# Retention followed by a Fourier-mix block: residual of two row blocks on VectorE, their rows earlier, and two loads placed behind the first weight

## The chip, the cores and the metric

The kernel runs on one core of a Trainium2 chip. The metric is device microseconds of one execution, as the median of the runs. The core's engines are named here as the profile names them: TensorE (PE, and PEld for its weight loads), VectorE (DVE), ScalarE (ACT), GpSimd (POOL), and SyncE (SP), which issues most of the DMAs. Each engine works through its own instructions in order and waits on semaphores of the others.

## The reference

Four batches of 768 rows; eight heads of 64 columns make rows of 512. The first half is a decaying linear attention, the second a Fourier mix with a normalisation and a two-layer network, all in float32:

```python
for t in range(S):                                   # attention, per head h, gamma[h]
    state = gamma * state + outer(k[t], v[t])
    y[t] = scale * q[t] @ state
x = heads of y side by side                          # [4, 768, 512]
X = np.fft.fft(np.fft.fft(x, axis=1), axis=2)
u = x + np.real(X)                                   # the residual x is added here
un = (u - mean(u)) / sqrt(var(u) + 1e-6)             # over the 512 columns
out = u + np.maximum(un @ w_ch1, 0) @ w_ch2          # 512 -> 2048 -> 512
```

## The kernel before

A batch is worked in this order: load and cast q, k, v by head pairs; transposes, scores, state and outputs of the attention, which fill `x` (float16, 768 rows as six chunks of 128); the Fourier transform over rows (stage one, giving four tables `g`), then over columns (stage two), which gives `u` for six row blocks of 128 rows, called row blocks 0 to 5 here (`kb` in the code). Row blocks 3 to 5 come from reversed copies of the tables, `g16r` (units `gr0` to `gr3`). Then each row block is normalised (`bn_stats`, `bn_aggr`, then `un = mean - u`), transposed to `unT`, and goes through the network: `psh = w1 * unT`, relu into `ht`, `psc = ht * w2`, and `ob = psc * (1/std) + u`, which is stored.

The first batch has code of its own, since nothing runs beside its beginning. Its instructions are emitted in the order of the string `FIRST`, and `pin()` makes each engine keep that order. The tokens that matter here:

- `sa<r><part>`: the stage-two matmuls of row block r (r = 0, 1, 2) into one PSUM tile `pq0`. Part 0, 2 and 3 multiply the tables; part 1 adds the residual x by two matmuls with an identity matrix.
- `ua<r>`: takes `pq0` out of PSUM to `u`, adding the per-row constant `g0` (L929 on ScalarE, L931 on VectorE).
- `bn<r>` (L953, L954) and `n<r>` (L963, on ScalarE): statistics and `un`. Row block 0 has a shortcut: its mean is known beforehand, so `nh0`, `nh1` (L943) make `un` straight from PSUM, `pt0`, `pt1` (L975) transpose it and `pe0`, `pe1` (L981) copy it to `unT`.
- `g0`, `g1`, `g2`: the three steps of the constant `g0` (DVE L874 and L882; nine small matmuls L891; DVE L897 and L900). `csn0` is a table copy that the nine matmuls need (L355).
- `ge01`, `ge11`: the last two tables `g` out of PSUM (L837). `gr0` to `gr3`: the reversed copies (L863, VectorE).
- `fs3`: the last fold of x (DVE L760), read by the stage-one matmuls `s011`, `s111` (L827).
- `w0` to `w7`: issue of the eight weight loads on GpSimd's queue, four for w_ch1 (L1144), four for w_ch2 (L1151). The loads for q, k and v go through SyncE's queue (L215 for the first batch, L195 for later ones).

Behind the first batch's string, units are merged by due times. For row blocks 0 to 2 of the first batch the up-projection is done per row block in four groups of 16 matmuls (`h0_unit`, L1104). I write (r, g) for group g of row block r. Each group fills one of three PSUM buffers (pool `ps_pm`), which is emptied by relu (L1111 on ScalarE for even g, L1113 on VectorE for odd g). Before row blocks 1 and 2 stands `unT_unit` (transposes L1074, copy L1076 on VectorE or L1078 on ScalarE). On ScalarE the eight scaled masks for later batches (L277, `late_consts`) are issued behind the last `un` of `FIRST`. Stage two of row blocks 3 to 5 (`s2_unit`: matmuls L1025 and L1028, ScalarE copy L1030, VectorE L1031 and L1033, residual on GpSimd L1037 and L1039), their statistics (L1049, L1050) and `un` (L1051) run among these groups. The down-projection (`psc`, L1130) uses the same three PSUM buffers.

The loads of q for the first two head pairs of the second batch are issued at the head of the program, directly behind the first batch's twelve loads:

```python
for name, i in LOADS0:
    first_load(name, i, nc.sync)()
load_unit(1, 0, None, "q")()
load_unit(1, 1, None, "q")()
```

The other loads of the second batch wait for weight load `w6` and for the last matmul of (1, 3).

Of the kernel before, what the change touches and what calls it, by code (L numbers as in the profile page):

```python
# [18 lines left out]
P = 128  # L19
# [19 lines left out]
yi11 t21 sc1 ae110@v yi10 fs0 fl2@g yx1 q3 s110 w0 k31@g e21@a x10@v am20 am21 x11@a fs1 ta40  # L39
v22@a s010 k30@a t30 e30@a t31 v21@g e31@a ae201@v ta30 ae200@v kv2 ae211@v yi21 ae210@v gk2@g  # L40
sc2 csn2@a w1 csn1@v am30 ae300@v ta31 yi20 yx2 v32@g x20@a ae301@v xs0@v x21@a ta41 fl3@a gk3@g
s100 am31 ae311@v s000 v31@g kv3 fs2 s101 ge10@a ae310@v w2 s001 w3 yi31 sc3 ge00@a yi30 yx3 g0
x30@a sa00 sa10 edge x31@v fs3 w4 gr0 sa11 csn0@v s011 xs2@a xs3@v w5 s111 xs1@a sa20 mean
ge01@a sa02 sa01 ge11@v sa03 nh0@a gr3 sa12 nh1@a gr1 sa13 g1 sa21 pt0 g2 ua1@v pt1 sa22 pe0@a
pe1@a w6 ua0@v bn1 sa23 ua2@a gr2 n1 bn2 n2 w7
"""
ON_ACT = {'q': (0, 1, 0), 'kv': (1, 1, 1), 'g': (0, 1, 1), 'gr': (0, 0, 0)}
FB = 1
# [13 lines left out]
def kernel(  # L62
# [122 lines left out]
    def load_unit(b, i, after=None, names="qkv"):  # L185
        def run():
            h0 = 2 * PAIR_ORDER[i]
            for name in names:
                if (name, b, i) in in_of:
                    continue  # L190
                src = srcs[name]
                t = inp.tile([P, 2, NCH, D], f32, tag="in32", name=f"{name}32")
                rows = "h (p c) d -> p h c d" if b < NPE and name == "q" else \
                    "h (c p) d -> p h c d"
                dma = nc.sync.dma_start(t, src[b, h0:h0 + 2].rearrange(rows, p=P))  # L195
                if after is not None:
                    for x in (w_dma[after].ins, lb[0]["mm"].ins):
# [19 lines left out]

    for name, i in LOADS0:
        first_load(name, i, nc.sync)()
    load_unit(1, 0, None, "q")()  # L220
    load_unit(1, 1, None, "q")()


    icol_i = const.tile([P, 8], i32, tag="icol_i")
# [679 lines left out]
    lb = {}  # L904

    def sa_unit(kb, part):
        def run():
            if part == 0:
                if 0 not in lb:
                    lb[0] = dict(u=up.tile([P, NCH, DM], f32, tag="u32", name="u32"),  # L910
                                 unT=up.tile([P, 4, S], f16, tag="unT", name="unT"),
                                 st=stt.tile([P, NCH, 4], f32, tag="stats", name="stats"))
                lb[0]["pq", kb] = ps_g.tile([P, DM], f32, tag="g", name="pq0")
            pq, g, x = lb[0]["pq", kb], fd[0]["g"], xts[0][:, kb]
            sl = slice(kb * P, kb * P + P)
            ops = (((g[:, 0, sl], cd16[:, 0], 0, DM), (g[:, 2, sl], sd16[:, 0], 0, DM)),
                   ((ident16, x[:, 0, 1:257], 0, 256), (ident16, x[:, 1, 257:1:-1], 256, DM)),
                   ((g[:, 1, sl], cd16[:, 1], 0, DM),),
                   ((g[:, 3, sl], sd16[:, 1], 0, DM),))[part]
            for n, (lhsT, rhs, c0, c1) in enumerate(ops):  # L920
                nc.tensor.matmul(pq[:, c0:c1], lhsT, rhs, start=(part == 0 and n == 0),  # L921
                                 stop=part == 3, skip_group_check=True)
        return run

    def ua_unit(kb, eng):
        def run():
            dst, src, g0 = lb[0]["u"][:, kb], lb[0]["pq", kb], fd[0]["g0"][:, kb:kb + 1]
            if eng == "a":
                nc.scalar.activation(dst, src, AF.Identity, bias=g0, scale=1.0)  # L929
            else:  # L930
                nc.vector.tensor_scalar(out=dst, in0=src, scalar1=g0, scalar2=0.0, op0=ALU.add,  # L931
# [162 lines left out]
                                        op0=ALU.mult, op1=ALU.max)  # L1094
        return run

    def h0_unit(kb, g):
        def run():
            unT = lb[0]["unT"]
            psh = ps_pm.tile([P, 4, P], f32, tag="pm", name="psh0")  # L1100
            for f in range(4):
                fb = 4 * g + f
                for cb in range(4):
                    mm = nc.tensor.matmul(psh[:, f], w116[:, cb, fb * P:(fb + 1) * P],  # L1104
                                          unT[:, cb, kb * P:(kb + 1) * P],
                                          start=(cb == 0), stop=(cb == 3))
# [81 lines left out]
    def first_unit(name):  # L1188
# [16 lines left out]
            return x0_unit(n[0], n[1], eng or "a")  # L1205
        if kind == "ge":
            return s1e_unit(n[0], n[1], eng or "a")
        if kind == "nh":
            return n0_unit(n[0], eng or "a")
        if kind == "pe":  # L1210
# [33 lines left out]
    def mix_units(b, kbs, s0, s1, u0, u1):  # L1244
        def turn(j):
            def run():
# [5 lines left out]
        return [([turn(j) for j in range(3)], s0, s1), ([norm_unit(b, kbs[2])], t, t),  # L1252
                ([unT_unit(b, kb) for kb in kbs], u0, u1)]

    def emit(streams):
        ev = []
        for si, (units, t0, t1) in enumerate(streams):
# [18 lines left out]
    for b in range(B):  # L1276
        majors = []
        if b == 0:
            for kb in range(3):
                if kb:  # L1280
                    majors.append(unT_unit(0, kb))
                majors += [h0_unit(kb, g) for g in range(4)]
        else:
            majors += [h_unit(b, 0, fb) for fb in range(NFB)]
        majors.append(rstd_unit(b, 0))
# [56 lines left out]
```

## Time and profile before

| | |
|---|---|
| median of 3 runs (lowest to highest) | 242.21 us (242.10 to 242.36) |
| the profiled execution | 242.18 us, of which its span 240.4 us |
| PE busy | 228.3 us, 95% of the span |
| DVE busy | 173.4 us, 72% |
| ACT busy | 120.8 us, 50% |
| POOL busy | 82.8 us, 34% |
| DMA, mean rate | 153 GB/s, 36.77 MB |

The profile is of one execution. Times in its views are counted from the start of the span; what lies around the span (1.8 us here) isn't shown. A row of the timeline has the start, the duration, the engine, the source line and the operation with its tiles; in square brackets stands how long the engine had been idle before it and what it waited for.

### The profile page before, as it was taken

What the parts mean: (1) busy time and instruction counts of PE and PEld (TensorE: products, weight loads), DVE (VectorE), ACT (ScalarE), POOL (GpSimd) and SP (SyncE); (2) the same over time, 40 slices, a digit from 0 to 9 for tenths busy, and PEclk for the clock granted to TensorE, in tenths of its full rate; (3) what the DMA queues carried; (4) which work ended last, traced back from release to release, by engine and by line L of the source; (5) the groups of instructions that cost most, each with busy time, mean ns of one, the idle gap of its engine ahead of it and who ended that gap; (6) DMA issues with size and microseconds to landing.
All of it is one profiled execution on the core that took longest, in us unless ns stands there. A gap on an engine that the chain in (4) does not pass through costs nothing.

```text
span 240.4 us, 5243 instructions
## 1 busy us (share of the span) xinstructions
PE 228.3 (95%) x1999; PEld 142.5 (59%) x1999; DVE 173.4 (72%) x421; ACT 120.8 (50%) x268; POOL 82.8 (34%) x151
## 2 busy tenths in 40 slices
PE   0988999999999999999999999999999999999994
PEld 0466779766774756665567446655675455446542
DVE  8999887958898789977895749977886557215121
ACT  5989758675864544931148406722366227203400
POOL 7678802675300197840002808920004124000000
PEclk9999999999999999999999999999999999999999
DMA  7999999999999289979999488675100331221012
GB/s 181 231 271 238 236 206 208 215 248 246 260 215 230 47 197 218 179 144 146 256 277 208 103 174 213 131 109 153 46 0 0 90 109 24 43 90 45 0 44 87
DMA packets 100808, 36.77 MB, mean 153 GB/s; under 512 B 91440, under 2 KB 97840, under 8 KB 100784
## 3 DMA queue, kind: packets, MB, share of 16 engines
q1 hardware_dynamic: 96560, 32.25, 63.2%
q0 software_dynamic: 4224, 4.19, 10.5%
q8 instruction: 15, 0.25, 0.5%
q14 instruction: 9, 0.07, 0.1%
HBM read 27.26 MB, written 6.29 MB: 140 GB/s over the span
## 4 chain that ended last, share of the span: by engine, by line
PE 85%; DVE 4%; DMA 3%; POOL 2%; ACT 2%; SPq 1%; issue 1%; ACTq 0%
PE psc L1130 34%; PE psh L1087 28%; PE psh L1104 3%; PE wkA L664 3%; DMA v<-in_v_dram 3%; PE ps L847 3%; PE wkY L718 2%; PE pq L1009 2%; PE ps L827 1%; PE wkY L714 1%; PE wkK L683 1%; PE pq L921 1%; SPq L215 1%; PE tq L620 1%; POOL q16z L453 1%
## 5 line engine op out<-in xcount | busy, mean ns | idle before, releaser
L1130 PE MATMUL psc<-w,ht 128*128 128x512 f16 (+2 forms) x400 | 88.9, 370 | 0.0
L1087 PE MATMUL psh<-unT,w 128*128 128x384 f16 x448 | 81.6, 326 | 0.3 <-ACT ht L1091 0.3
L1130 PEld LDWEIGHTS <-ht 128*128 128x128 f16 x400 | 37.6, 98 | 36.7
L1087 PEld LDWEIGHTS <-w 128*128 128x128 f16 x448 | 42.1, 98 | 24.2 <-issue 0.8
L1091 ACT ACTIVATE ht<-psh 128x384 f16<-128x384 f32 x66 | 31.7, 490 | 41.2 <-PE psh L1087 40.6
L1037 POOL TENSOR_TENSOR u<-u,x 128x256 f32<-128x256 f32 x21 | 13.3, 635 | 107.8 <-DVE u L1016 95.6
L1134 DVE SCALAR_TENSOR_TENSOR ob<-psc,stats,u 128x512 f32<-128x512 f32 (+2 forms) x25 | 18.1, 725 | 29.2 <-PE psc L1130 29.0
L1093 DVE TENSOR_SCALAR ht<-psh 128x384 f16<-128x384 f32 x46 | 25.3, 550 | 8.9 <-PE psh L1087 8.4
L667 DVE TENSOR_TENSOR atm<-wkA,maskp 128x512 f16<-128x512 f32 x36 | 23.6, 681 | 1.5 <-PE wkA L664 1.5
L1051 ACT ACTIVATE un<-u,stats 128x512 f16<-128x512 f32 x21 | 14.9, 719 | 12.2 <-DVE stats L1050 8.2
L1049 DVE BATCH_NORM_STATS2 bst<-u 128x6 f32<-128x512 f32 x21 | 14.5, 688 | 4.9 <-POOL u L1039 4.7
L693 DVE SCALAR_TENSOR_TENSOR s<-s,gk,wkK 128x128 f16<-128x128 f16 x48 | 16.2, 337 | 2.4 <-ACT s L689 1.6
L726 ACT ACTIVATE x<-wkY,gexp 128x384 f16<-128x384 f32 x24 | 12.9, 581 | 9.0 <-PE wkY L718 8.9
L438 POOL TENSOR_SCALAR kd<-k,gexp 128x384 f16<-128x384 f32 x24 | 13.8, 586 | 3.3 <-DMA k<-in_k_dram 3.1
L664 PE MATMUL wkA<-qTz,kT 128*128 128x256 f16 x72 | 13.2, 272 | 0.1
L1039 POOL TENSOR_TENSOR u<-u,x 128x256 f32<-128x256 f32 x21 | 13.3, 635 | 0.0
L1011 ACT COPY qn<-pq 128x128 f32<-128x128 f32 x18 | 4.9, 274 | 13.7 <-PE pq L1009 13.7
L1104 PEld LDWEIGHTS <-w 128*128 128x128 f16 x192 | 11.0, 98 | 0.9 <-issue 0.6
L1104 PE MATMUL psh<-unT,w 128*128 128x128 f16 x192 | 11.4, 219 | 0.1
L1016 DVE SCALAR_TENSOR_TENSOR u<-pq,g,qn 128x256 f32<-128x256 f32 x18 | 8.5, 474 | 3.2 <-PE psh L1087 2.5
L443 POOL TENSOR_SCALAR v<-v 128x768 f16<-128x768 f32 x12 | 10.0, 832 | 1.6 <-DMA v<-in_v_dram 1.6
L664 PEld LDWEIGHTS <-kT 128*128 128x128 f16 x72 | 6.9, 98 | 5.7 <-issue 0.6
(177 smaller groups left out, 311.9 us busy)
## 6 DMA issues: line engine op xcount, KB each, us to landing
q<-in_q_dram SPq DMA_DIRECT2D x16, 384.0 KB, 6.1
k<-in_k_dram SPq DMA_DIRECT2D x16, 384.0 KB, 5.4
v<-in_v_dram SPq DMA_DIRECT2D x16, 384.0 KB, 6.0
out_dram<-ob SPq DMA_DIRECT2D x23, 256.0 KB, 2.4
w<-in_moe_w_ch_dram POOLq DMA_DIRECT2D x8, 512.0 KB, 10.9
unT<-un SPq DMA_TRANSPOSE x15, 2.4
out_dram<-ob SPq DMA_DIRECT2D x1, 192.0 KB, 1.9
kT<-kd SPq DMA_TRANSPOSE x10, 3.0
```

Of the source, the lines that this page charges most:

```text
L438: kc = nc.gpsimd.tensor_scalar(out=kd[:, :, h2, :], in0=k32[:, h2], scalar1=gkd[:, h0 + h2:h0 + h2 + 1], scalar2=1.0, op0=ALU.mult, op1=AL ...
L664: mm = nc.tensor.matmul(wk[:, c2], st["kT"][:, c, :], st["qT"][:, :, c, :], start=True, stop=True)
L667: nc.vector.tensor_tensor(out=st["atm"][:, 2 * part:2 * part + 2], in0=wk, in1=maskp[:, PAIR_ORDER[i]].unsqueeze(1).to_broadcast([P, 2, 2, ...
L693: nc.vector.scalar_tensor_tensor(out=s16[:, c], in0=s16[:, c - 1], scalar=gk2[:, hp:hp + 1], in1=wk[:, c - c0], op0=ALU.mult, op1=ALU.add)
L1049: nc.vector.bn_stats(bst, u[:, kb, :])
L1051: nc.scalar.activation(un, u[:, kb, :], AF.Identity, bias=stats[:, kb, 0:1], scale=-1.0)
L1087: nc.tensor.matmul(psh, w116[:, cb, fb * P:(fb + 1) * P], unT[:, cb, rt * 384:(rt + 1) * 384], start=(cb == 0), stop=(cb == 3))
L1091: nc.scalar.activation(ht16[:, fb, :], psh, AF.Relu, bias=0.0, scale=-1.0)
L1093: nc.vector.tensor_scalar(out=ht16[:, fb, :], in0=psh, scalar1=-1.0, scalar2=0.0, op0=ALU.mult, op1=ALU.max)
L1104: mm = nc.tensor.matmul(psh[:, f], w116[:, cb, fb * P:(fb + 1) * P], unT[:, cb, kb * P:(kb + 1) * P], start=(cb == 0), stop=(cb == 3))
L1130: nc.tensor.matmul(psc[:, c0:c1], ht16[:, fb, rb3 * P:(rb3 + 1) * P], w216[:, fb, c0:c1], start=(fb == 0), stop=(fb == NFB - 1))
L1134: nc.vector.scalar_tensor_tensor(out=ob[:, c0:c1], in0=psc[:, c0:c1], scalar=lb[b]["st"][:, rb, 3:4], in1=lb[b]["u"][:, rb, c0:c1], op0=AL ...
```

## The change

- Row blocks 1 and 2 of the first batch no longer get their residual by identity matmuls (`sa11` and `sa21` are gone from `FIRST`). `ua1` and `ua2` now are two `scalar_tensor_tensor` each on VectorE, of 128x256, which read PSUM, add `g0` and add x; the second reads x backwards. Row block 0 keeps the identity matmuls, and its `ua0` moves from VectorE to ScalarE, while `ua2` moves from ScalarE to VectorE.
- The order in `FIRST` is another: `csn0` and `g1` are earlier; `g2`, `sa12`, `sa13`, `ua1` and `bn1` come directly behind row block 0's last matmul; all four `gr` copies come at the end, behind `bn2`.
- `unT_unit(0, 1)` and `unT_unit(0, 2)` are emitted in the middle of the group before their row block (after two of its four parts), and a unit that does nothing keeps the count of units as it was. In the program that results, TensorE's order around the first three row blocks is: (0,0), (0,1), (0,2); transposes of row block 1; transposes of row block 2; two matmuls of row block 3's stage two; (0,3); four matmuls of row blocks 3 and 4; (1,0) to (1,3); (2,0); the other six matmuls of row blocks 4 and 5; (2,1) to (2,3). Before it was: (0,0), (0,1), (0,2); three transposes; (0,3); five transposes; all twelve matmuls of row blocks 3 to 5; (1,0) to (2,3). Later, in the second half of the first batch's network, some matmuls of the second batch's attention and of the network change places.
- The two early q loads of the second batch are no longer at the head of the program. They stand in `FIRST` as `lq02` and `lq13`: the first waits until weight load `w2` has landed, the second until `w3` has.

```diff
-s100 am31 ae311@v s000 v31@g kv3 fs2 s101 ge10@a ae310@v w2 s001 w3 yi31 sc3 ge00@a yi30 yx3 g0
-x30@a sa00 sa10 edge x31@v fs3 w4 gr0 sa11 csn0@v s011 xs2@a xs3@v w5 s111 xs1@a sa20 mean
-ge01@a sa02 sa01 ge11@v sa03 nh0@a gr3 sa12 nh1@a gr1 sa13 g1 sa21 pt0 g2 ua1@v pt1 sa22 pe0@a
-pe1@a w6 ua0@v bn1 sa23 ua2@a gr2 n1 bn2 n2 w7
+s100 am31 ae311@v s000 v31@g kv3 fs2 s101 ge10@a ae310@v w2 s001 w3 lq02 yi31 sc3 ge00@a yi30
+csn0@v yx3 g0 x30@a sa00 sa10 g1 edge x31@v fs3 w4 lq13 s011 xs2@a xs3@v w5 s111 xs1@a sa20 mean
+ge01@a sa02 sa01 ge11@v g2 sa03 sa12 sa13 ua1@v bn1 nh0@a nh1@a pt0 pt1 sa22 pe0@a pe1@a n1 w6
+ua0@a sa23 ua2@v bn2 gr3 gr1 gr0 gr2 n2 w7
...
     for name, i in LOADS0:
         first_load(name, i, nc.sync)()
-    load_unit(1, 0, None, "q")()
-    load_unit(1, 1, None, "q")()
...
     def ua_unit(kb, eng):
         def run():
             dst, src, g0 = lb[0]["u"][:, kb], lb[0]["pq", kb], fd[0]["g0"][:, kb:kb + 1]
-            if eng == "a":
+            if kb:
+                x = xts[0][:, kb]
+                for c0, r in ((0, x[:, 0, 1:257]), (256, x[:, 1, 257:1:-1])):
+                    nc.vector.scalar_tensor_tensor(out=dst[:, c0:c0 + 256],
+                                                   in0=src[:, c0:c0 + 256], scalar=g0, in1=r,
+                                                   op0=ALU.add, op1=ALU.add)
+            elif eng == "a":
...
-    def h0_unit(kb, g):
+    def h0_unit(kb, g, between=None):
         def run():
             unT = lb[0]["unT"]
             psh = ps_pm.tile([P, 4, P], f32, tag="pm", name="psh0")
             for f in range(4):
                 fb = 4 * g + f
+                if f == 2 and between:
+                    between()
...
+        if kind == "lq":
+            return load_unit(1, n[0], n[1], "q")
...
             for kb in range(3):
-                if kb:
-                    majors.append(unT_unit(0, kb))
-                majors += [h0_unit(kb, g) for g in range(4)]
+                majors += [h0_unit(kb, g, unT_unit(0, kb + 1) if kb < 2 and g == 3 else None)
+                           for g in range(4)] + [done] * (kb < 2)
```

More of the change, by code (lines that the diff above doesn't have):

```diff
@@ L196, in run @@
                 if after is not None:
-                    for x in (w_dma[after].ins, lb[0]["mm"].ins):
+                    for x in [w_dma[after].ins] + ([lb[0]["mm"].ins] if "mm" in lb[0] else []):
                         tc.add_manual_dep(dma.ins, x.name,
@@ L902, in g0_c @@
         fd[b]["g0"] = g0.rearrange("p a k -> p (a k)")
-    lb = {}
+    lb = {0: {}}
     def sa_unit(kb, part):
@@ L908, in run @@
             if part == 0:
-                if 0 not in lb:
-                    lb[0] = dict(u=up.tile([P, NCH, DM], f32, tag="u32", name="u32"),
+                if "u" not in lb[0]:
+                    lb[0].update(u=up.tile([P, NCH, DM], f32, tag="u32", name="u32"),
                                  unT=up.tile([P, 4, S], f16, tag="unT", name="unT"),
@@ L1253, in mix_units, with done @@
                 ([unT_unit(b, kb) for kb in kbs], u0, u1)]
+    def done():
+        pass
     def emit(streams):
```

## The prediction

> **What bounds the kernel now.** I read the page first, then the busy time by stretches, then the timeline of PE, ACT and DVE from 28 to 46 us, where the change lies.
>
> ```profile
> span 240.4 us, 5243 instructions
> ...
> PE 85%; DVE 4%; DMA 3%; POOL 2%; ACT 2%; SPq 1%; issue 1%; ACTq 0%
> ```
>
> ```profile
> 46.00:60.00 14.00, 14.00 (x127) 8.51 (x125) 10.43 (x30) 9.53 (x16) 8.40 (x12) 1.00 1.22 246
> ```
>
> The second fence is one row of the busy time by stretches; its columns are the stretch, its length, then PE, PEld, DVE, ACT, POOL, granted clock, DMA share, GB/s. PE is busy for 14.00 of 14.00 us, at full clock, and the chain that ended last is PE for 85% of the span. So what the change does before 46 us reaches the end as the shift of one event: the start of the first down-projection, `psc`, at 45.49. The sum is made for that start and added to the profiled execution's own 242.18 us (span 240.4), which is within 0.03 of the median, 242.21.
>
> ```profile
> 28.06 0.38 PE L921 MATMUL pq<-x,ident 128*128 128x256 f16 x2
> ...
> 29.00 0.66 PE L827 MATMUL ps<-ssn,xab 128*128 128x193 f16 x6
> ...
> 30.43 0.39 PE L921 MATMUL pq<-sd,g 128*128 128x512 f16 x1
> ...
> 31.09 0.37 PE L891 MATMUL ps<-xg,csn 128*128 128x4 f16 x9
> 31.32 0.38 PE L921 MATMUL pq<-x,ident 128*128 128x256 f16 x2
> 31.54 0.50 PE L975 MATMUL pst<-ident,un 128*128 128x128 f16 x4
> ...
> 32.50 3.00 PE L1104 MATMUL psh<-unT,w 128*128 128x128 f16 x48
> 35.34 0.33 PE L1074 MATMUL pst<-ident,un 128*128 128x128 f16 x3
> 35.72 1.05 PE L1104 MATMUL psh<-unT,w 128*128 128x128 f16 x16
> 36.61 0.44 PE L1074 MATMUL pst<-ident,un 128*128 128x128 f16 x5
> 36.89 0.38 PE L1025 MATMUL pq<-cd,g16r 128*128 128x257 f16 x2
> ...
> 38.35 7.31 PE L1104 MATMUL psh<-unT,w 128*128 128x128 f16 x128
> 45.49 0.81 PE L1130 MATMUL psc<-w,ht 128*128 128x512 f16 x3
> ```
>
> Starts give the prices on PE: an identity pair 0.22 (31.32 to 31.54), a group of 16 matmuls 0.89 (35.72 to 36.61), five transposes 0.28 (36.61 to 36.89), two stage-two matmuls of 257 columns as much as the identity pair of 256, 0.22, and the eight groups from 38.35 to 45.49 7.1 us. The first group doesn't wait for PE's own work but for ScalarE's copy to `unT`; (0,3) at 35.72 waits for VectorE's relu of (0,1), and (1,0) at 38.35 for ScalarE's relu of (0,0). Those chains are these, ScalarE's first, then VectorE's:
>
> ```profile
> 30.86 0.84 ACT L943 ACTIVATE un<-pq,mu 128x256 f16<-128x256 f32 x2 [1.06 <-DVE g16r L863]
> 32.08 0.65 ACT L981 COPY unT<-pst 128x256 f16<-128x256 f16 x2 [0.38 <-PE pst L975]
> ...
> 34.16 0.72 ACT L963 ACTIVATE un<-u,stats 128x512 f16<-128x512 f32 x1 [0.85 <-DVE stats L954]
> 35.50 0.72 ACT L963 ACTIVATE un<-u,stats 128x512 f16<-128x512 f32 x1 [0.61 <-DVE stats L954]
> 36.13 1.69 ACT L277 ACTIVATE maskp<-maskf 128x128 f32<-128x128 f32 x8
> ...
> 40.60 0.37 ACT L1030 COPY qn<-pq 128x255 f32<-128x255 f32 x1 [0.31 <-DVE u L1033]
> ```
>
> ```profile
> 29.79 0.58 DVE L837 CAST g<-ps 128x386 f16<-128x386 f32 x1
> ...
> 31.90 1.41 DVE L931 TENSOR_SCALAR u<-pq,g 128x512 f32<-128x512 f32 x2
> ...
> 34.05 0.23 DVE L863 COPY g16r<-g 128x384 f16<-128x384 f16 x1
> 34.19 0.69 DVE L953 BATCH_NORM_STATS2 bst<-u 128x6 f32<-128x512 f32 x1
> 34.91 0.18 DVE L954 BATCH_NORM_AGGREGATE stats<-bst 128x2 f32<-128x6 f32 x1
> 35.01 0.66 DVE L1113 TENSOR_SCALAR ht<-psh 128x512 f16<-128x512 f32 x1
> ...
> 39.64 0.49 DVE L1031 SCALAR_TENSOR_TENSOR u<-pq,g,qn 128x257 f32<-128x257 f32 x1 [0.91 <-ACT qn L1030]
> 40.04 0.47 DVE L1033 SCALAR_TENSOR_TENSOR u<-pq,g,qn 128x255 f32<-128x255 f32 x1
> ```
>
> **The change, part by part.**
>
> *To the first group.* The last table copy (L837, 29.79) stood behind other work of VectorE; the matmuls that feed it ended at 29.66 (29.00 + 0.66). With `gr0` and `csn0` out of its way it can gain 0 to 0.13. The matmul that it releases stands at 30.43, behind other work of PE, so I take the middle, 0.06: `un` at 30.80, the first group at 32.44.
>
> *The identity matmuls.* Four leave: 0.44 us of PE. Between 0 and 0.44 of it could show. I take 0 for this place. The first pair's slot (28.06) goes to the nine small matmuls, which cost 0.23 (31.09 to 31.32); where the second pair and those nine stood, PE now runs row block 1's last two matmuls (30.59 to 31.03) and then waits for the first half of `un` (30.80 + half of 0.84) until about 31.3. ScalarE's chain, not PE, ends last here.
>
> *VectorE up to the relu of (0,1).* Row block 1's tile is complete at 31.19 (30.81 + 0.38). `ua1` can start at 31.22 instead of 31.90: the two small steps of `g0`, which stood between the matmuls of 31.09 and 31.90, now fit between the table copy and that. It costs more: two instructions that the trace doesn't have in this form. The nearest rows are L1031 and L1033, also from PSUM with a second tensor: 0.40 between starts, so 0.87 for a row block. The cheapest bound is half of L931's pair, 0.70. I take 0.87. Then with 0.69 and 0.18 for the statistics: `ua1` to 32.09, `bn1` to 33.02, `ua2` to 33.82 (0.87 where ScalarE did it before), `bn2` to 34.76, four `gr` copies of 0.23 (one stood here before) to 35.5, relu of (0,1) to 36.09. Before it ended at 35.67: 0.42 later. (0,3) starts at 36.14.
>
> *ScalarE up to the relu of (0,0).* The `un` of row block 1 runs from 33.05, `ua0`, as large as one of L931's two, takes 0.70 to 34.4, `un` of row block 2 starts at 34.79 instead of 35.50. From there to (1,0) took 2.85 before (35.50 to 38.35: the masks, the relu, the release). So (1,0) may start at 37.64, 0.71 earlier.
>
> *PE between.* The 48 matmuls end at 35.28 (32.44 + 2.84). Four transposes, 0.22; the next four wait for ScalarE until 35.56 and end at 35.78; two stage-two matmuls to 36.00; a wait to 36.14; (0,3) to 37.03; four stage-two matmuls to 37.47; a wait to 37.64. Then 7.1 for the eight groups and 0.66 for the six stage-two matmuls that now stand behind (2,0): PE is free at 45.40, 0.09 before the old start.
>
> *The PSUM buffer of the first `psc`.* It is that of (2,2), released by ScalarE's relu. In ScalarE's order that relu stands behind `un` of row block 3, which needs a VectorE result that now stands behind L1031 and L1033 of row block 4; and row block 4's matmuls now come behind (2,0), which ends at 42.08. From there: two matmuls done at 42.46; ScalarE's relu of (2,0), then its copy (0.37) to 43.14; VectorE, which has the relu of (1,3) to 42.05 and then two statistics to 43.34, does L1031 and L1033 to 44.13 and the aggregate to 44.24; `un` to 44.98; relu to 45.50; `psc` at 45.53. So 0.04 later than 45.49 in place of 0.09 earlier.
>
> *Behind that.*
>
> ```profile
> 44.82 0.83 POOL L428 TENSOR_SCALAR q16z<-q 128x768 f16<-128x768 f32 x1
> ...
> 45.76 1.39 ACT L1051 ACTIVATE un<-u,stats 128x512 f16<-128x512 f32 x2 [0.36 <-DVE stats L1050]
> ...
> 50.70 0.39 PE L1074 MATMUL pst<-ident,un 128*128 128x128 f16 x4
> ```
>
> Row blocks 4 and 5 get their `un` about 1.3 us later than 47.15 (45.76 + 1.39). PE transposes row block 4 at 50.70 and row block 5 behind that, which covers it.
>
> *The q loads.* First their issues, then two of the weight loads with the time to landing, then the sizes:
>
> ```profile
> 16.63 4.19 SPq L195 DMA_DIRECT2D q<-in_q_dram  x2
> ```
>
> ```profile
> L1144 POOL DMA_DIRECT2D w<-in_moe_w_ch_dram x2: 747/773/799, 24.3 to 25.1; - x2
> ...
> DMA to landing us min/median/max: 8.2/9.1/10.0
> ```
>
> ```profile
> q<-in_q_dram SPq DMA_DIRECT2D x16, 384.0 KB, 6.1
> ...
> w<-in_moe_w_ch_dram POOLq DMA_DIRECT2D x8, 512.0 KB, 10.9
> ```
>
> Two issues leave SyncE's queue at 16.63 and wait for `w2` (24.3 + 8.2 = 32.5 before) and `w3` (25.1 + 10.0 = 35.1). Behind them on SyncE stands a k load that waits for `w6` and the end of (1,3), which come later than `w3`, so nobody there is delayed. Their first reader is GpSimd's cast at 44.82; a load that took 10.0 us from 32.5 would be there at 42.5, and that slack hides the move. The weights may come up to a few us sooner, but the first group waits for ScalarE and not for `w0`: 0 in the sum.
>
> Sum: -0.09 + 0.13 = +0.04, so 242.18 + 0.04 = 242.2 us: no change that can be told. A measurement of this kernel tells some 0.2%, 0.48 us, from no change.
>
> **Rivals.**
>
> *The waits I put in are not there.* If the new VectorE instructions cost 0.70 a row block, and ScalarE and VectorE run 0.3 us ahead of my reckoning, PE never waits for (0,3), (1,0) or `psc`: 45.40 less 0.14 less 0.17 and less the 0.06 behind the first four transposes is 45.03, a gain of 0.46; with the rest of the 0.13 at the table copy 0.53, so 241.65 us. It decides where the relu of (0,0) ends before 37.2. For it: less work on PE is real. Against it: VectorE's list has 0.42 more in front of that relu.
>
> *ScalarE's waits for two engines cost more (slower).* Before the `un` at 35.50 ScalarE had been idle for 0.61, and its operand was there at 35.09 (34.91 + 0.18); it started 0.41 after that.
>
> ```profile
> L963 ACTq EVENT_SEMAPHORE  x1: 17/17/17, 35.1 to 35.1; - x1
> ```
>
> This wait stood in an instruction of its own at 35.1. In the changed program the relu of (0,0) has such a pair of waits. If it costs the same 0.41, (1,0) starts at 38.05 and all behind it moves; if it comes again at `un` of row block 3, ahead of the buffer for `psc`, it is 0.82: 242.6 to 243.0, as one figure 242.8. It decides from some 0.45 in all. Against it: at 40.60 and 45.76 ScalarE started within 0.1 of the operand. The Trainium skill, Perfetto Trace Analysis, Identifying Dependency Chains, says that an instruction that waits on several engines may get extra semaphore instructions ahead of it; it gives no price, and this trace shows both 0.41 and under 0.1.
>
> *The fourth weight comes late (slower).* (0,3) needs `w3`, which landed at 35.1 with no q load beside it. Now the first q load (384 KB) runs beside `w3`. The weights of 512 KB landed some 2.5 us apart (32.5, 35.1), so q's share is up to 1.9: `w3` at 37.0, (0,3) 0.9 late, 243.1 us. It decides if `w3` lands after 36.1. Against it: the early q loads no longer run beside `w0` and `w1`, which should bring all weights forward as much. The Trainium skill, DMA: Bandwidth & Descriptors, Issuing engines are not separate DMA queues, says that loads of all issuing engines run on the same 16 DMA engines and interleave. By that rule both halves hold, the share that q takes from `w3` and the share it gives back before.
>
> That the q loads' move does nothing is contained in the forecast.
>
> **How the numbers follow.** Forecast (within 0.48 us): 0.48. Waits gone: 0.22, the chance of faster. ScalarE's waits 0.24 and the late weight 0.06: slower 0.30. The likeliest case gives 242.2. The range must reach into both other cases: down past 241.65 by 0.3 for later waits that the changed order behind 60 us may remove or add, 241.3; up to 243.0, the far end of the ScalarE case. That leaves out less than 2 in 10.
>
> **What would show it.** Right: L931's successor at about 31.2 with 0.4 between starts; `un` of row block 2 at 34.8; (0,3) near 36.1 and (1,0) near 37.6; `psc` at 45.3 to 45.7 behind ScalarE; PE full after it. Wrong: (1,0) before 37.3 or after 38.0, `psc` before 45.0 or after 46.0, a PE wait for `w3`, or idle PE behind 46 us.

## The result and the profile after

| | before | after |
|---|---|---|
| median (lowest to highest), 16 runs each | 242.28 us (241.89 to 243.14) | 243.02 us (242.25 to 244.01) |
| ratio to before, 95% interval | | 1.0026 (1.0016 to 1.0036) |
| the profiled execution, its span | 242.18 us, 240.4 | 242.57 us, 240.8 |

The changed kernel is slower by 0.26%, some 0.6 us. The profiled execution after is the sixth fastest of its 16, so its trace shows 0.39 us of a loss that is 0.74 between the medians. What the slower executions lose beyond that is in no trace of this kernel.

The page of the changed kernel: the span, and the chain that ended last by engine.

```profile
span 240.8 us, 5237 instructions
...
PE 71%; DMA 9%; DVE 8%; ACT 4%; POOL 3%; issue 2%; SPq 1%; ACTq 0%; POOLq 0%; DVEq 0%
```

PE went from 85% to 71% of that chain and DMA from 3% to 9%: the chain that ended last now runs over transfers more often. First the stretch that the prediction worked out, the timeline of PE, VectorE and ScalarE in the changed kernel (L1110 is the up-projection, L1136 `psc`, L929 the new `ua1` and `ua2`, L1119 and L1117 the relus, L967 and L1055 `un`):

```profile
32.69 3.00 PE L1110 MATMUL psh<-unT,w 128*128 128x128 f16 x48
...
36.32 1.05 PE L1110 MATMUL psh<-unT,w 128*128 128x128 f16 x16
...
37.89 4.63 PE L1110 MATMUL psh<-unT,w 128*128 128x128 f16 x80
...
45.81 0.59 PE L1136 MATMUL psc<-w,ht 128*128 128x512 f16 x2
```

```profile
31.48 0.88 DVE L929 SCALAR_TENSOR_TENSOR u<-pq,g,x 128x256 f32<-128x256 f32 x2 [0.67 <-PE pq L919]
...
33.22 0.84 DVE L929 SCALAR_TENSOR_TENSOR u<-pq,g,x 128x256 f32<-128x256 f32 x2
...
35.58 0.69 DVE L1119 TENSOR_SCALAR ht<-psh 128x512 f16<-128x512 f32 x1
```

```profile
35.04 0.72 ACT L967 ACTIVATE un<-u,stats 128x512 f16<-128x512 f32 x1 [0.41 <-DVE stats L958]
35.67 1.69 ACT L275 ACTIVATE maskp<-maskf 128x128 f32<-128x128 f32 x8
37.27 1.05 ACT L1117 ACTIVATE ht<-psh 128x512 f16<-128x512 f32 x2
...
44.55 0.72 ACT L1055 ACTIVATE un<-u,stats 128x512 f16<-128x512 f32 x1 [0.86 <-DVE stats L1054]
45.18 0.58 ACT L1117 ACTIVATE ht<-psh 128x512 f16<-128x512 f32 x1
```

Each event has the place and the releaser that the prediction gave it, and each is late by about the same: `ua1` 31.48 for 31.22, `un` of row block 2 35.04 for 34.79, (1,0) 37.89 for 37.64, `psc` 45.81 for 45.53. The 0.25 was there before all of them. It begins at 22.7, at a place that the prediction did not consider. The timeline of VectorE and GpSimd there, of before and then of after:

```profile
22.66 0.36 DVE L355 COPY csn<-csp 128x384 f16<-128x384 f16 x1
...
23.02 0.50 POOL L479 TENSOR_SCALAR v<-v 128x384 f16<-128x384 f32 x1 [0.64 <-DMA v<-in_v_dram]
```

```profile
22.55 0.50 POOL L477 TENSOR_SCALAR v<-v 128x384 f16<-128x384 f32 x1
...
22.70 0.60 DVE L353 COPY csn<-csp 128x384 f16<-128x384 f16 x1
```

Before, GpSimd waited 0.64 us for the last `v` half and cast it when VectorE's table copy was done. After, no q load (issued at 16.63 before) runs beside that v load's tail, the v tile lands 7.7 us after its issue instead of 8.2, the cast is issued ahead of the copy, and the copy takes 0.60 instead of 0.36. What waits for VectorE is some 0.25 late from there on.

The second place is behind 46 us. SyncE's issues, of before and of after:

```profile
42.86 0.37 SPq L195 DMA_DIRECT2D k<-in_k_dram  x1
```

```profile
31.67 2.94 SPq L195 DMA_DIRECT2D q<-in_q_dram  x2
44.26 0.37 SPq L195 DMA_DIRECT2D k<-in_k_dram  x1
```

The q loads now stand behind `w2` and `w3`, two of the four loads of the first weight, and the first k load of the second batch, which waits for `w6`, is issued 1.4 us later. Weight loads `w5`, `w6`, `w7`, issues and time to landing, of before and of after:

```profile
L1151 POOL DMA_DIRECT2D w<-in_moe_w_ch_dram x3: 770/780/790, 26.6 to 28.1; - x3
...
DMA to landing us min/median/max: 13.6/15.4/17.2
```

```profile
L1157 POOL DMA_DIRECT2D w<-in_moe_w_ch_dram x3: 770/780/790, 26.3 to 27.8; - x3
...
DMA to landing us min/median/max: 15.3/17.1/18.9
```

`w6` is the middle one: 27.4 + 15.4 = 42.8 before, 27.0 + 17.1 = 44.1 after. Why it is later shows in the busy time by stretches (the last three columns are PE's granted clock, the mean busy share of the DMA engines and GB/s), of before and of after:

```profile
18.00:24.00 6.00, 5.38 (x93) 3.92 (x90) 5.65 (x14) 5.72 (x12) 4.99 (x10) 1.00 1.25 238
24.00:30.00 6.00, 5.98 (x77) 4.33 (x78) 5.13 (x17) 4.46 (x11) 4.88 (x9) 1.00 1.21 237
30.00:36.00 6.00, 5.92 (x81) 4.48 (x79) 5.15 (x14) 3.30 (x7) 0.00 (x0) 1.00 1.24 206
36.00:42.00 6.00, 6.00 (x97) 5.72 (x95) 4.59 (x12) 5.26 (x17) 1.65 (x3) 1.00 1.24 207
```

```profile
18.00:24.00 6.00, 5.37 (x91) 3.91 (x88) 5.64 (x13) 5.70 (x12) 5.52 (x11) 1.00 1.17 185
24.00:30.00 6.00, 5.90 (x84) 4.41 (x83) 5.12 (x17) 4.44 (x12) 4.55 (x9) 1.00 1.21 196
30.00:36.00 6.00, 5.75 (x70) 4.04 (x68) 5.16 (x16) 3.80 (x10) 0.00 (x0) 1.00 1.21 205
36.00:42.00 6.00, 5.92 (x100) 5.64 (x98) 4.61 (x11) 4.18 (x13) 0.95 (x2) 1.00 1.18 252
```

From 18 to 30 us the transfers moved 12 us x some 47 GB/s = 0.56 MB less; from 30 to 36 they moved as much as before, and from 36 to 42 they made up 6 x 45 = 0.27 MB. The rest, 0.29 MB, is some 1.4 us at the 206 GB/s that after has from 42 to 44 us. Over half of the 0.56 MB is lost in the two microseconds from 20 to 22, where before moved 276 GB/s at a busy share of 1.19 and after 121 at 0.92: `w1` is issued only at 21.6, and without the q loads the engines had less to do there. Who pays is in the timeline of GpSimd and PE (of before, then of after): the last of the second batch's k tiles is cast at 62.05 instead of 60.56, its DMA transpose `kT` follows, and PE's scores wait for it.

```profile
60.56 1.15 POOL L438 TENSOR_SCALAR kd<-k,gexp 128x384 f16<-128x384 f32 x2 [0.82 <-DMA k<-in_k_dram]
...
65.86 0.82 PE L664 MATMUL wkA<-qTz,kT 128*128 128x256 f16 x6
```

```profile
62.05 1.15 POOL L436 TENSOR_SCALAR kd<-k,gexp 128x384 f16<-128x384 f32 x2 [0.81 <-DMA k<-in_k_dram]
...
66.13 0.83 PE L662 MATMUL wkA<-qTz,kT 128*128 128x256 f16 x6 [0.43 <-DMA kT<-kd]
```

That is the new idle time of PE, 0.43 us, where before had none between 46 and 76 us. With the front's 0.32 (45.49 to 45.81) it makes 0.75; 0.39 came out; of the difference, 0.3 is a delay of PE near 116 us that before has and after has not, told of below.

### The profile page after: what moved, and what is told of

It is laid out like the page before. It is cut to its first block, busy times and chain, and to the rows that moved or that the text cites. A ratio compares the mean times of both kernels' runs of the same rounds, so it can differ in the third digit from the quotient of the medians.

```text
span 240.8 us, 5237 instructions
## 1 busy us (share of the span) xinstructions
PE 227.5 (94%) x1995; PEld 142.3 (59%) x1995; DVE 173.5 (72%) x423; ACT 120.2 (50%) x268; POOL 82.9 (34%) x151
## 4 chain that ended last, share of the span: by engine, by line
PE 71%; DMA 9%; DVE 8%; ACT 4%; POOL 3%; issue 2%; SPq 1%; ACTq 0%; POOLq 0%; DVEq 0%
PE psc L1136 29%; PE psh L1091 25%; DMA v<-in_v_dram 3%; PE ps L845 3%; DMA k<-in_k_dram 3%; PE wkA L662 3%; DMA q<-in_q_dram 2%; DMA kT<-kd 2%; PE pq L1013 2%; PE psh L1110 2%; PE wkY L716 2%; PE ps L825 1%; PE wkY L712 1%; SPq L215 1%; PE wkK L681 1%
## 5 line engine op out<-in xcount | busy, mean ns | idle before, releaser
L1136 PE MATMUL psc<-w,ht 128*128 128x512 f16 (+2 forms) x400 | 88.9, 370 | 0.0
L1136 PEld LDWEIGHTS <-ht 128*128 128x128 f16 x400 | 37.7, 98 | 36.8
L1055 ACT ACTIVATE un<-u,stats 128x512 f16<-128x512 f32 x21 | 14.9, 719 | 14.4 <-DVE stats L1054 10.4
L1110 PE MATMUL psh<-unT,w 128*128 128x128 f16 x192 | 11.5, 219 | 0.1
L1110 PEld LDWEIGHTS <-w 128*128 128x128 f16 x192 | 11.1, 98 | 0.9 <-issue 0.6
```

What stands on the lines that cost most here:

```text
L1055: nc.scalar.activation(un, u[:, kb, :], AF.Identity, bias=stats[:, kb, 0:1], scale=-1.0)
L1136: nc.tensor.matmul(psc[:, c0:c1], ht16[:, fb, rb3 * P:(rb3 + 1) * P], w216[:, fb, c0:c1], start=(fb == 0), stop=(fb == NFB - 1))
```

## The experiments

**Theory A** after the comparison: the whole loss comes from the q loads' move, 0.25 us by the copy beside the cast and 0.4 to 0.5 by the late k tiles. **Theory B**: it comes from the new VectorE residual and the new order. Each ratio below is to the kernel before in the same comparison, with its 95% interval.

**e1, everything but the q loads' move**

```diff
     for name, i in LOADS0:
         first_load(name, i, nc.sync)()
+    load_unit(1, 0, None, "q")()
+    load_unit(1, 1, None, "q")()
...
-s100 am31 ae311@v s000 v31@g kv3 fs2 s101 ge10@a ae310@v w2 s001 w3 lq02 yi31 sc3 ge00@a yi30
-csn0@v yx3 g0 x30@a sa00 sa10 g1 edge x31@v fs3 w4 lq13 s011 xs2@a xs3@v w5 s111 xs1@a sa20 mean
+s100 am31 ae311@v s000 v31@g kv3 fs2 s101 ge10@a ae310@v w2 s001 w3 yi31 sc3 ge00@a yi30
+csn0@v yx3 g0 x30@a sa00 sa10 g1 edge x31@v fs3 w4 s011 xs2@a xs3@v w5 s111 xs1@a sa20 mean
```

> The changed kernel with the two early q loads back at the head of SyncE's queue, everything else of the change kept. Theory A (the loss of 0.6 to 0.7 us comes from the q loads' move alone: 0.25 us by a VectorE copy at 22.7 that runs beside a GpSimd cast and takes 0.60 instead of 0.36, and 0.4 to 0.5 us by k loads of the second batch that start 1.4 us later and make PE wait at 66): the copy takes 0.36 again, first psc at 45.55, first k load at 42.9, no PE wait at 66, ratio to before 0.999 to 1.001 (242.1 to 242.5 us). Theory B (the loss comes from the new VectorE residual and the new order of row blocks): ratio 1.002 to 1.003, 242.8 to 243.0 us, k load at 42.9 all the same.

242.03 us (241.90 to 242.14, 12 runs), ratio 0.9984 (0.9975 to 0.9994). Timelines of VectorE and PE in e1:

```profile
22.77 0.36 DVE L355 COPY csn<-csp 128x384 f16<-128x384 f16 x1
```

```profile
32.53 3.00 PE L1112 MATMUL psh<-unT,w 128*128 128x128 f16 x48
...
45.66 1.67 PE L1138 MATMUL psc<-w,ht 128*128 128x512 f16 x7
```

The copy takes 0.36 again, the first k load leaves at 43.15 (0.3 later than in before, 1.1 sooner than in the changed kernel), and PE has no wait near 66. Theory B falls: without the q loads' move the change is not slower but 0.16% faster. The gain isn't made before 46 us, where `psc` comes 0.17 later than in before. Its fastest run is no faster than that of before (241.90 to 241.88 in this comparison); what it lacks is the longer ones, and its runs lie within 0.24 us of each other.

**e2, the q loads' move alone**

```diff
     for name, i in LOADS0:
         first_load(name, i, nc.sync)()
-    load_unit(1, 0, None, "q")()
-    load_unit(1, 1, None, "q")()
...
-s100 am31 ae311@v s000 v31@g kv3 fs2 s101 ge10@a ae310@v w2 s001 w3 yi31 sc3 ge00@a yi30 yx3 g0
-x30@a sa00 sa10 edge x31@v fs3 w4 gr0 sa11 csn0@v s011 xs2@a xs3@v w5 s111 xs1@a sa20 mean
+s100 am31 ae311@v s000 v31@g kv3 fs2 s101 ge10@a ae310@v w2 s001 w3 lq02 yi31 sc3 ge00@a yi30 yx3 g0
+x30@a sa00 sa10 edge x31@v fs3 w4 lq13 gr0 sa11 csn0@v s011 xs2@a xs3@v w5 s111 xs1@a sa20 mean
```

> The kernel before with nothing changed but the two early q loads, moved behind the third and fourth weight load. Theory A: the copy at 22.7 takes 0.60, first psc at 45.74 (45.49 + 0.25), first k load at 44.3, PE waits 0.4 to 0.5 us for the transposed k near 66; ratio 1.002 to 1.003, 242.7 to 243.0 us. Theory B: 0.999 to 1.001.

Shown are the lines that move the loads; those that make `lq` a token are as in the changed kernel. 242.99 us (242.12 to 245.03, 12 runs), ratio 1.0026 (1.0006 to 1.0046), the same as the whole change. First k load 44.64. PE's waits from 60 to 120 us:

```profile
PE wkA L662 <- DMA kT<-kd: 0.4, 1, 0.4
PE wkA L662 <- DMA qTz<-q16z: 0.3, 1, 0.3
```

The copy took 0.53. But `psc` came at 45.69, and e5 below, whose front is that of before, had the same 45.69 with a copy of 0.36. So in the old order of the front the copy's delay does not show, as far as one profile of each can tell, and what this profile has beyond that of e5 is the wait of 0.4 for the k tile; in the new order the copy's delay does show (next). The wait for `qTz` is the one near 116 us, which is no loss against before.

**e3, the changed kernel, the cast behind the copy**

```diff
                 last_cast[0, i] = nc.gpsimd.tensor_scalar(
...
+                if (i, part) == (3, 2):
+                    tc.add_manual_dep(last_cast[0, i].ins, csn_of[1].ins.name,
+                                      mybir.DependencyInfo(mybir.DependencyClass.Sync,
+                                                           mybir.DependencyReason.DATA),
+                                      reason="cast behind the copy")
```

> The changed kernel with one wait more: GpSimd's cast of the last v half (22.55 in the changed kernel) waits for VectorE's copy of 22.7, so the two do not run at the same time. Theory A: the copy takes 0.36, first psc near 45.55 (0.25 earlier than the 45.81 of the changed kernel), k load still at 44.3 and the PE wait near 66 still there and if anything longer by the 0.25, since the loads do not move with PE; total 242.75 to 243.0, between the two kernels. If the copy still takes 0.60, the neighbour on GpSimd is not what slows it, and psc stays at 45.8.

242.86 us (242.51 to 243.92, 12 runs), ratio 1.0016 (0.9998 to 1.0034). Timelines of VectorE and PE, and PE's wait from 60 to 76 us:

```profile
22.76 0.36 DVE L354 COPY csn<-csp 128x384 f16<-128x384 f16 x1
```

```profile
32.52 3.00 PE L1119 MATMUL psh<-unT,w 128*128 128x128 f16 x48
```

```profile
PE wkA L671 <- DMA kT<-kd: 1.0, 1, 1.0
```

With the two kept apart (the cast starts at 23.23) the copy takes 0.36 and the first group starts 9.76 us behind the copy's start (32.52 - 22.76), as in e1 (9.76), not 9.99 as in the changed kernel: the cast beside it is what costs 0.23. Runs with a longer copy bear it out: in e4 below it takes 0.68, 0.32 more than alone, and the first group starts 10.08 behind the copy's start, 0.32 more than 9.76; in e7 1.34 and 10.74, both 0.98 more. PE arrives sooner at the k tiles and waits longer for them, as expected, by more than the 0.25 expected, since the k load is later too (44.52). The run times alone don't tell: the interval holds no change from before as well as the loss of the changed kernel.

**e4, the changed kernel, k and v loads behind `w5`**

```diff
-                streams.append(([load_unit(1, i, 6) for i in range(4)], LD0[0], LD0[1]))
+                streams.append(([load_unit(1, i, 5) for i in range(4)], LD0[0], LD0[1]))
```

> The changed kernel with the second batch's k and v loads waiting for the sixth weight load (w5, landed at 41.6) instead of the seventh (w6, 44.1). Theory A: first k load near 41.7, the k tiles transposed 1.5 us or more sooner, no PE wait at 66: 0.4 to 0.5 us faster than the changed kernel, 242.5 to 242.6 us, with first psc still at 45.8. Against it: the k and v loads now share the DMA engines with w6 and w7, and if a down-projection then waits for w7 it is no faster. Theory B: same as the changed kernel, 243.0.

242.69 us (242.28 to 243.02, 12 runs), ratio 1.0005 (0.9993 to 1.0016): faster than the changed kernel in the median, though not for the reason given. The loads begin at 42.64, 1.6 sooner, but the last k tile comes no sooner (GpSimd, then PE's wait):

```profile
62.38 1.16 POOL L436 TENSOR_SCALAR kd<-k,gexp 128x384 f16<-128x384 f32 x2 [0.89 <-DMA k<-in_k_dram]
```

```profile
PE wkA L662 <- DMA kT<-kd: 0.6, 1, 0.6
```

So an earlier issue doesn't bring the k tile sooner. That the transfers ahead of it have lost time, and that an earlier start only lets them share it with `w6` and `w7`, fits the rates but is argued, not tested. The run times show no loss against before, although this profile has both the slow copy and the wait; why, the trace does not show.

**e7, the q loads behind `w0` and `w1`**

```diff
-s100 am31 ae311@v s000 v31@g kv3 fs2 s101 ge10@a ae310@v w2 s001 w3 lq02 yi31 sc3 ge00@a yi30
-csn0@v yx3 g0 x30@a sa00 sa10 g1 edge x31@v fs3 w4 lq13 s011 xs2@a xs3@v w5 s111 xs1@a sa20 mean
+s100 am31 ae311@v s000 v31@g kv3 fs2 s101 ge10@a ae310@v w2 s001 w3 lq00 lq11 yi31 sc3 ge00@a yi30
+csn0@v yx3 g0 x30@a sa00 sa10 g1 edge x31@v fs3 w4 s011 xs2@a xs3@v w5 s111 xs1@a sa20 mean
```

> The changed kernel with the two early q loads waiting for the first and second weight load (w0 landed at 24.9, w1 at 27.9) instead of the third and fourth. If the loss is DMA time left unused while the weights run alone, the first k load comes between 43.1 and 44.3, near 43.7, and the PE wait near 66 goes down from 0.43 to 0.1 or nothing; the VectorE copy at 22.7 still takes 0.60, since the v load still has no q load beside it, so first psc stays at 45.8. Total between e1 and the changed kernel, 242.3 to 242.7 us. If only where the loads are issued matters and not the unused time, the same as the changed kernel, 243.0.

243.23 us (241.99 to 243.96, 12 runs), ratio 1.0027 (1.0011 to 1.0043): no better. The q loads left at 25.14, yet the rate was 182 and 176 GB/s in the stretches from 18 and from 24 us and 251 only from 30, and the first k load came at 44.41. What is lost is lost by 30 us; the 43.7 expected, between the two kernels, was wrong. VectorE and GpSimd in the profiled execution:

```profile
22.77 1.34 DVE L353 COPY csn<-csp 128x384 f16<-128x384 f16 x1
```

```profile
22.53 0.53 POOL L477 TENSOR_SCALAR v<-v 128x384 f16<-128x384 f32 x1
23.00 0.41 POOL L269 COPY gk<-gk 128x256 f32<-128x256 f32 x1
23.36 0.51 POOL L477 TENSOR_SCALAR v<-v 128x384 f16<-128x384 f32 x1
```

Here the copy got through only behind the third GpSimd instruction: 24.11, 0.24 after 23.87. In the changed kernel it ended at 23.30, 0.25 after the end of the first (23.05). `psc` was at 46.63, and PE, so much later, waited only 0.2 us for `kT`.

**e12, two k loads at the head instead of the q loads**

```diff
     for name, i in LOADS0:
         first_load(name, i, nc.sync)()
+    load_unit(1, 0, None, "k")()
+    load_unit(1, 1, None, "k")()
```

> The changed kernel (q loads still behind the third and fourth weight load) with two other loads in the place that the q loads had: the first two k loads of the second batch, of 384 KB too, issued at the head. If the loss of the changed kernel is DMA time left unused beside the first weights, any two loads at the head repair it: 235 GB/s or so from 18 to 30 us, the last v half lands late again, so that VectorE's copy at 22.7 takes 0.36, first v load of the second batch near 42.9, no PE wait for kT near 66; 242.0 to 242.3 us, as e1. If the loss comes from the q tiles themselves being late (GpSimd casts q first for each pair), it stays: 242.8 to 243.1.

243.03 us (242.85 to 243.19, 6 runs), ratio 1.0033 (1.0021 to 1.0046). Half of the expectation came: the copy took 0.36, the first group started at 32.43, PE had no idle time from 64 to 68. But fewer bytes moved from 18 to 24 us at a higher share (221 GB/s at 1.32, where before had 238 at 1.25), and the weights came late. PE's waits from 30 to 76 us:

```profile
PE psh L1112 <- DMA w<-in_moe_w_ch_dram: 0.9, 1, 0.9
...
PE psc L1138 <- DMA w<-in_moe_w_ch_dram: 0.3, 1, 0.3
```

So this run confirms that a load at the head keeps the cast off the copy. It doesn't settle the wait near 66: the last k tile is cast at 61.46, between the two kernels (60.56 and 62.05), and PE itself is late, with `psc` at 46.38. Nor does it tell whether the q tiles' own lateness costs anything. It is also the rival with the late fourth weight, at the 0.9 that the prediction gave it, in another kernel.

**e8, the residual on VectorE alone, old order, q loads at the head**

```diff
-x30@a sa00 sa10 edge x31@v fs3 w4 gr0 sa11 csn0@v s011 xs2@a xs3@v w5 s111 xs1@a sa20 mean
-ge01@a sa02 sa01 ge11@v sa03 nh0@a gr3 sa12 nh1@a gr1 sa13 g1 sa21 pt0 g2 ua1@v pt1 sa22 pe0@a
-pe1@a w6 ua0@v bn1 sa23 ua2@a gr2 n1 bn2 n2 w7
+x30@a sa00 sa10 edge x31@v fs3 w4 gr0 csn0@v s011 xs2@a xs3@v w5 s111 xs1@a sa20 mean
+ge01@a sa02 sa01 ge11@v sa03 nh0@a gr3 sa12 nh1@a gr1 sa13 g1 pt0 g2 ua1@v pt1 sa22 pe0@a
+pe1@a w6 ua0@v bn1 sa23 ua2@v gr2 n1 bn2 n2 w7
...
+            if kb:
+                x = xts[0][:, kb]
+                for c0, r in ((0, x[:, 0, 1:257]), (256, x[:, 1, 257:1:-1])):
+                    nc.vector.scalar_tensor_tensor(out=dst[:, c0:c0 + 256],
+                                                   in0=src[:, c0:c0 + 256], scalar=g0, in1=r,
+                                                   op0=ALU.add, op1=ALU.add)
```

> The kernel before with only the residual of row blocks 1 and 2 moved to VectorE (four identity matmuls gone, ua2 on VectorE); first string otherwise in its old order, q loads at the head, no transposes in the middle of a group. The planner puts SyncE in the same order as in e1. Theory C: 242.0 to 242.2 us whatever the first psc does, if that lies within 0.2 of 45.5. If the new order of the first string is worth something, first psc is later here than e1's 45.66, by up to 0.4 (row block 1's statistics stand behind the two long VectorE steps of row blocks 0 and 1), 242.2 to 242.5. If the residual alone is worth its 0.44 us of PE: psc at 45.1, 241.6 us.

242.81 us (242.70 to 243.09, 11 runs), ratio 1.0016 (1.0007 to 1.0025). PE:

```profile
36.95 1.05 PE L1110 MATMUL psh<-unT,w 128*128 128x128 f16 x16 [0.91 <-DVE ht L1119]
```

(0,3) waits 0.91 us for VectorE's relu, which stands at 36.24 behind `ua1`, `ua0` (L937, still VectorE's) and `ua2`; `psc` comes at 46.71. The new order, which gives `ua0` to ScalarE and puts `g2` and `ua1` forward, buys that back: in e1 the relu starts at 35.42 and `psc` at 45.66. The 0.44 us that the identity matmuls took on PE are lost in that wait.

**e5 and e6, SyncE's order.** With the new front the planner also moved three outputs on SyncE one place back. **Theory C**: this is what makes e1 faster than before. **Theory D**: it is not. e5 is the kernel before with that order (shown in part), e6 is e1 with the old one, by the same pairs reversed and one pair more:

```diff
+    for x, y in ((("out", 0, 3), ("v", 2, 2)), (("out", 0, 4), ("qT", 2, 0)),
+                 (("out", 0, 5), ("k", 2, 3))):
+        tc.add_manual_dep(sp_of[x].ins, sp_of[y].ins.name,
+                          mybir.DependencyInfo(mybir.DependencyClass.NoSync,
+                                               mybir.DependencyReason.DATA),
+                          reason="order on SyncE")
```

> The kernel before, with only three instructions of SyncE's queue in another place, as the changed kernel has them: the outputs of row blocks 3, 4 and 5 of the first batch stand one place later, behind the third v load, the first qTz transpose and the fourth k load of the third batch. All other engines keep their order. Theory C (the 0.35 us by which e1 beats before come from this order on SyncE, which the planner changed as a by-product): the qTz transpose at 109 is issued in 2.5 instead of 4.1 us, PE no longer waits 0.28 near 116, 241.9 to 242.1 us with little spread, ratio 0.998 to 0.999. Theory D (they come from the new work on PE, VectorE and ScalarE before 46 us): no change, 1.000, 242.3 us.

> e1 (the changed kernel with q loads at the head) with those three outputs back in the places they have in the kernel before; nothing else. Theory C: qTz transpose at 109 takes 4.1 us again, PE waits 0.28 near 116, the spread of the runs is back, 242.3 to 242.6 us, ratio 1.000 to 1.001, since its first psc is 0.17 later than before. Theory D: as e1, 242.03 us, ratio 0.9985.

e5: 242.31 us (241.95 to 242.73, 11 runs), ratio 1.0000 (0.9989 to 1.0011). e6: 242.01 us (241.90 to 242.13, 11 runs), ratio 0.9987 (0.9978 to 0.9996). Theory C falls in both. What differs between e1 and before does sit near 116 us: the DMA transpose `qTz` there, of before and of e1 (in e5 it took 4.09 us to issue, in e6 2.70):

```profile
L609 SPq DMA_TRANSPOSE qTz<-q16z x1: 4139/4139/4139, 109.2 to 109.2; - x1
...
DMA to landing us min/median/max: 6.8/6.8/6.8
```

```profile
L609 SPq DMA_TRANSPOSE qTz<-q16z x1: 2541/2541/2541, 109.3 to 109.3; - x1
...
DMA to landing us min/median/max: 6.2/6.2/6.2
```

In before it lands at 109.2 + 6.8 = 116.0, and the scores that read it start at 116.16, 2.89 us behind the start of the twelve `psc` matmuls ahead of them (113.27); in e1 it lands at 115.5, and the scores start 2.59 behind (113.37 to 115.96). So before loses 0.3 us there; only in the profiles of e2 and e7 does the list of waits name this one. The short form is in the profiles of the changed kernel and of e1, e3, e4, e6, e8, e10, e11 and e12, the long one in before, e2, e5 and e7: three of these four have the old front, but e7 the new one, and e8 has the old order of the front with the short form. What decides between them is open, and with it what makes e1 faster; SyncE's order is not it.

**e10, one VectorE instruction moved in e1**

```diff
+    for x, y in ((("u", 4), ("aggr", 3)),):
+        tc.add_manual_dep(at_of[x].ins, at_of[y].ins.name,
+                          mybir.DependencyInfo(mybir.DependencyClass.NoSync,
+                                               mybir.DependencyReason.DATA),
+                          reason="statistics first")
```

> e1 with one VectorE instruction moved: the aggregate of row block 3's statistics (44.13 in e1) stands ahead of the two PSUM steps of row block 4. If the first psc waits for the relu of (2,2) behind the un of row block 3, as the prediction's last step had it, un comes near 43.6 instead of 44.4, and psc is set by PE alone: 45.53 instead of 45.66, 0.13 sooner, 241.9 us. If that relu is not what releases psc, no change: 45.66, 242.03.

241.94 us (241.81 to 242.54, 11 runs), ratio 0.9987 (0.9978 to 0.9995). PE:

```profile
42.96 2.84 PE L1113 MATMUL psh<-unT,w 128*128 128x128 f16 x48
45.64 1.67 PE L1139 MATMUL psc<-w,ht 128*128 128x512 f16 x7
```

`un` of row block 3 starts at 43.72 on ScalarE, and `psc` now follows the last groups after 2.68 us, with nothing between; in e1 it was 2.81 (42.85 to 45.66). The 0.13 that the prediction gave to this wait is what moving one instruction takes away behind the last groups; the start of `psc` itself (45.64 for 45.66) moves less, since the first group came 0.11 later in this execution (32.64 for 32.53). It is the fastest version here by its median, though its gain over e1 is too small to tell from none.

**e11, e10 with ScalarE's masks behind the relu of (1,0)**

```diff
-    for x, y in ((("u", 4), ("aggr", 3)),):
+    for x, y in ((("u", 4), ("aggr", 3)), ("mask", ("relu", 1, 0))):
```

> e10 with ScalarE's eight masks (1.69 us from 35.52 in e1, ahead of the relu of (0,0)) behind the relu of (1,0). (1,0) then waits for nothing: it starts at 37.05 behind (0,3) instead of 37.73, with the matmuls of row blocks 3 and 4 behind it; all waits of PE before psc are gone, so that psc comes 0.35 to 0.4 before e1's, near 45.3: 241.6 to 241.7 us, ratio 0.997. If the masks now hold up a later relu or un, psc stays at 45.5 to 45.7 and the time at 241.9 to 242.1.

242.56 us (242.45 to 242.64, 11 runs), ratio 1.0014 (1.0006 to 1.0023). A miss: with the masks gone from there the planner put PE in another order, (0,3) started at 36.63 instead of 36.16, `un` of row block 3 at 44.93 and `psc` at 46.23.

## Why the prediction was wrong

The forecast was no change, 242.2 us; it is slower by 0.26%. e1 and e2 show that the q loads' move is the cause; the split of the loss between the copy and the k tiles is read from profiles. In order of the prediction's steps:

- *To the first group*, -0.06: it came at 32.69 for 32.44. The step's own terms hold within the spread: in e1 and e3 the first group starts 9.76 us behind the copy's start at 22.7, in before 9.84 (32.50 - 22.66), in e5, with the same front as before, 9.94. What it lacked is the copy itself, slowed by GpSimd's cast, +0.23. The prediction had written that the weights may come sooner and that this is 0 in the sum; that the first batch's last v half also comes sooner, and what GpSimd does with it, it did not ask.
- *The identity matmuls*, 0: nothing speaks against it. Without them and without the collision, in e1, `psc` starts 22.89 us behind the copy's start (45.66 - 22.77), in before 22.83 (45.49 - 22.66).
- *VectorE up to the relu of (0,1)*: right. 0.88 and 0.84 for a row block where 0.87 was taken; from the start of `ua1` to the relu's end 4.79 us (31.48 to 36.27) for 4.87.
- *ScalarE up to the relu of (0,0)*, and *PE between*: right, with the offset of the front: (1,0) at 37.89 for 37.64, (0,3) at 36.32 for 36.14.
- *The PSUM buffer of the first `psc`*: right in mechanism and size, as e10 shows: 0.13.
- *Behind that*: right as far as it goes, PE is full from 46 to 60 us; the second part of the loss came at 66.
- *The q loads*, 0: **the step that failed**. "Nobody there is delayed" considered the wait on SyncE, where the k load waits for `w6` anyhow, and took `w6` as fixed or sooner. It landed 1.3 us later, as the transfers ran at 185 instead of 238 GB/s from 18 to 24 us, where the q loads had been. The 0.23 of the copy comes of the same move. The slack that was reckoned was that of the q tiles' reader; the one that ran out belongs to the fourth k tile, whose PE reader at 66 had under 1.1 us of it: cast and transpose 1.5 us later, 0.43 of wait. e4 shows that this is not the whole account: its k tile is as late and its median has no loss.

Of the rivals, the waits of ScalarE for two engines did not come: its relu at 37.27 starts with the masks' end, and `un` of row block 2 at 35.04 starts 0.04 behind its operand (34.82 + 0.18) where before had 0.41. The fourth weight was not late (24.8 + 9.4 = 34.2 where 37.0 was feared). Their 242.8 and 243.1 lie near the measured time by chance, since neither cause occurred. For the late weight the prediction had cited the Trainium skill, DMA: Bandwidth & Descriptors, Issuing engines are not separate DMA queues: the loads of all issuing engines run on the same 16 DMA engines and interleave. The trace agrees: `w0` landed at 24.9 instead of 27.6 without q beside it. What the prediction made of it, that q gives back before as much as it takes later, doesn't hold: from 18 to 30 us fewer bytes moved in all. The list of signs had the right one as its last entry, idle PE behind 46 us, with no price.

The spread stays open. The changed kernel ran from 242.25 to 244.01 us, e3 without the collision from 242.51 to 243.92, before from 241.88 to 243.79 in the comparison of e1 to e4, and e1 from 241.90 to 242.14. The collision can be longer than in the profile (1.34 us in e7), but e3 shows that it isn't the whole of the spread.

On the copy, the Trainium skill, SBUF — State Buffer, Who interferes with whom, says that VectorE in a mode that uses two ports and GpSimd share one pair of ports, and that whichever issues second is blocked until the first has finished. The runs agree that the first holds up the second: the copy ended 0.25 after the end of the GpSimd instruction ahead of it in the changed kernel and 0.24 after the third in e7, and e3, which changes only who goes first, gave 0.36. Blocked from its first moment, a copy of 0.36 would have ended 0.36 after; so part of it passes beside the cast. That this copy runs in such a mode no run here shows.

## What to carry to other kernels

A load that is moved has two prices: what it meets at its new place, and what the transfers lose at the old one, if what is left there moves fewer bytes in the time; look at the GB/s of the stretch that it leaves, in slices of some 2 us. An operand that comes sooner can cost time too: ask which engine starts on it at once, and what its neighbour is doing then. Of a bundle of edits, price and try each alone: here everything but the q loads' move gained 0.16%, that move alone lost 0.26%, and the residual on VectorE alone, without the new order, lost 0.16%.

## What the runs showed of the hardware

- From 18 to 24 us the transfers moved 182 to 187 GB/s without q loads there (changed kernel, e2, e3, e4, e7) and 238 to 268 with them (before, e1, e5, e6, e8). The weight loads alone moved 206 and 207 GB/s in before from 30 to 42 us, at a share of 1.24, and with a q load beside them the changed kernel moved 252 from 36 to 42, at 1.18.
- One VectorE copy of 128x384 took 0.36 us where GpSimd's cast began behind it (before, e1, e3) and 0.53 (e2), 0.60 (changed kernel), 0.68 (e4) or 1.34 us (e7) where the cast began ahead of it.
- One DMA transpose of the same size, issued within 2 us of the same time, took 2.5 to 2.9 us to issue in nine profiles and 4.0 to 4.3 in four.
